# Attention key tiles of 128 rows per head, with the casts of q, k and v on VectorE and ScalarE

## The chip, the cores and the metric

The kernel runs on one core of a Trainium2 chip. The metric is device time in microseconds (us) of one launch. The engines are TensorE (PE, matmuls; its weight loads are PEld), VectorE (DVE), ScalarE (ACT), GpSimd (POOL) and SyncE (SP, which here only issues DMAs).

## The reference

Attention with a relative-position bias over 8 batch rows, 8 heads, 576 positions and head size 64; then a routed expert layer with 8 experts.

```python
scores = scale * np.matmul(q, k.transpose(0, 1, 3, 2))
...
bias = bias_table[bucket]            # bucket of |i - j|, 32 buckets, the last one from 128 on
scores = scores + bias.transpose(2, 0, 1)[None, :, :, :]
scores = scores - np.max(scores, axis=-1, keepdims=True)
attn = np.exp(scores)
attn = attn / (np.sum(attn, axis=-1, keepdims=True) + 1e-09)
return np.matmul(attn, v)
...
expert_idx = token_ids * np.int64(2654435761) % np.int64(E)
for e in range(E):
    h = np.maximum(x[expert_idx == e] @ w1[e], 0.0)
    out[expert_idx == e] = h @ w2[e]
```

q, k and v are float32 of shape (8, 8, 576, 64), w1 is (8, 512, 1024), w2 is (8, 1024, 512), and the output is float32 (4608, 512).

## The kernel before

There are two stages. The attention stage goes over 32 pairs of heads: a batch row and two heads, m and m + 4, whose 64 dimensions together fill the 128 partitions. The expert stage then goes over 8 experts with up to 640 tokens each.

**Attention, pair n.** load(n) (L176) brings q and k of the two heads as float32 on the SP queue, two rows of 64 to a packet of 512 bytes, four pairs ahead. cast_qk (L203) makes float16 of them on POOL. transpose_q (L321) and transpose_k (L337) turn them on PE in six blocks of 96 rows each, and VectorE copies the result out of PSUM: q as it is (L329), k into kz (L346). kz holds zeros where a key column belongs to the other head, so that one matmul over 128 partitions gives the scores of keys of both heads: a key tile of 128 columns is 64 keys of one head and 64 keys of the other, in an order where the even and odd positions of the sequence are kept apart.

The scores come out with keys on partitions and queries along the free dimension. scores(n, g) makes two key tiles at a time for g = 0 to 3 (L370, L374) and the last half tile for g = 4 (L385), into a PSUM tile ps of three banks with two buffers. ScalarE takes the exp (L378, L390) into att and atts. The bias is added as a factor: far from the diagonal the bias is one number per head, which cancels in the softmax, so only a band near the diagonal is multiplied, on VectorE (L411, and L417 for the last half tile), with ebd, the exp of the bias differences.

av_steps(n) multiplies att by va (L439): va holds v of both heads in float16 beside a column of ones each, 2 x 65 = 130 columns, with zeros in the rows of the other head. So 9 matmuls of 130 columns per tile of 128 queries, 45 per pair, give the numerators and the row sums; VectorE takes the reciprocals (L449) and scales into x_all (L450). The PSUM tiles px, pq and pk share two banks called aux. load_v (L188) brings v from the POOL queue, cast to float16 by the DMA, in packets of 64 values.

**Order.** All engines' orders in this stage are written out by hand. In the loop pass n, five score tiles of pair n alternate with 13, 14, 9 and 9 of the value matmuls of pair n - 1 on PE; transpose_k(n + 1) stands behind the first score tile and transpose_q(n + 2) behind the fourth. On VectorE the passes run: copy of k, band of the last half tile of pair n - 1, normalising of the first three query tiles, bands 0 and 1 of pair n, copy of q, band 2, normalising of the last two query tiles, band 3.

**The start.** The bias differences are made by a small matmul (bps) and an exp on ScalarE (ebsb), and written to DRAM by ScalarE's queue as t_f, shifted by one element per row (L535). Four DMAs on the SP queue read them back in diagonals as ebd (L549). z_init and va_init write zeros and ones on VectorE.

**Routing** is worked out on VectorE during passes 6 to 11. From pass 12 on, dispatch (L465) scatters finished rows of x_all to their expert's rows in DRAM (t_xperm) by indirect DMAs of POOL; the weights of the first two experts are loaded from POOL's queue in passes 20 to 28. route_load (L219) brings the token ids on SP in pass 4, and fill_table (L571) fills t_xperm on SP in passes 2 to 11. The last dispatches follow the last pair; then the expert stage loads its rows (L661), transposes them (L675), multiplies by w1 (L696), takes the relu (L702), multiplies by w2 (L714), and scatters the result (L722).

Of the kernel before, what the change touches and what calls it, by code (L numbers as in the profile page):

```python
# [11 lines left out]
F32 = mybir.dt.float32  # L12
# [19 lines left out]
def kernel(  # L32
# [11 lines left out]
    nc = tc.nc  # L44
# [63 lines left out]
    PW = 2 * FY + D // 2  # L108
    F_d = nc.dram_tensor("t5_f", [H * D + 1, PW], F16, kind="Internal")
# [36 lines left out]
    VW = 2 * (D + 1)  # L146
# [4 lines left out]
    with tc.tile_pool(name="at", bufs=1) as at, tc.tile_pool(  # L151
# [3 lines left out]
        def aux(shape, dtype, name):  # L155
# [4 lines left out]
        kz = [at.tile([P, NCH, 2, D], F16, name=f"kz{i}") for i in range(3)]  # L160
        va = [at.tile([P, NPAIR * NCH, VW], F16, name=f"va{i}")
              for i in range(2)]
        ebd = at.tile([P, NPAIR, 2, 2, WB], F16, name="ebd")
        te = at.tile([P, NGT], I32, name="te")
# [4 lines left out]
        qf, kf, qh, kh = {}, {}, {}, {}  # L169

        def load(n):
            b, m = pairs[n]
            for dst, src, name in ((qf, q, "qf"), (kf, k, "kf")):
                dst[n] = at.tile([PB, 2, NBLK, 2 * D], F32, name=name, bufs=4)
                for hh in range(2):
                    nc.sync.dma_start(  # L176
                        out=dst[n][:, hh, :, :],
                        in_=src[b, m + NPAIR * hh].rearrange(
                            "(k p c) d -> p k (c d)", k=NBLK, c=2
                        ),  # L180
                    )

        def load_v(b, m0, m1):
            for hh in range(2):
                for c in range(2):
                    r0 = D * hh + HD * c
                    c0 = hh * (D + 1)
                    nc.gpsimd.dma_start(  # L188
                        out=va[b % 2][r0 : r0 + HD, NCH * m0 : NCH * m1,
                                      c0 : c0 + D],  # L190
                        in_=bass.AP(
                            v.tensor,
                            (b * H + hh * NPAIR + m0) * S * D + c * D,
                            [[2 * D, HD], [D * D, NCH * (m1 - m0)], [1, D]],
                        ),
                    )

        def cast_qk(n, keng=None):
            for dst, src, name, eng in (
                (qh, qf, "qh", nc.gpsimd), (kh, kf, "kh", keng or nc.gpsimd)  # L200
            ):
                dst[n] = at.tile([PB, 2 * NBLK, 2, D], F16, name=name, bufs=3)
                eng.tensor_copy(  # L203
                    out=dst[n][:, :, :, :].transpose([0, 2, 1, 3]),
                    in_=src[n][:, :, :, :].rearrange(
                        "p h k (c d) -> p h (k c) d", c=2
                    ),
                )

# [122 lines left out]
        def transpose_k(n):  # L332
            pk = aux([P, S], F16, "pk")
            for k3 in range(NBLK):
                for c in range(2):
                    o = HALF * c + PB * k3
                    nc.tensor.transpose(  # L337
                        out=pk[:, o : o + PB],
                        in_=kh[n][:, 2 * k3 + c, :, :].rearrange(
                            "p h d -> p (h d)"  # L340
                        ),
                        identity=ident[:PB, :PB],
                    )
            z = kz[n % 3]
            for hh in range(2):
                nc.vector.tensor_copy(  # L346
                    out=z[D * hh : D * hh + D, :, hh, :].rearrange(
                        "p x (c u) -> p x c u", c=2
                    ),
                    in_=pk[D * hh : D * hh + D, :].rearrange(  # L350
                        "p (c x u) -> p x c u", c=2, u=HD
                    ),
                )
            ktz[n] = z

        def scores(n, g):
# [10 lines left out]
            if g < NDUO:  # L367
                for c in range(2):
                    kt = z[:, 2 * g + c, :, :].rearrange("p h u -> p (h u)")
                    nc.tensor.matmul(  # L370
                        out=ps[:, c, :QW], lhsT=kt, rhs=qt[:, :QW],
                        start=True, stop=True,
                    )
                    nc.tensor.matmul(  # L374
                        out=ps[:, 2, RW * c : RW * c + RW], lhsT=kt,
                        rhs=qt[:, QW:], start=True, stop=True,
                    )
# [4 lines left out]
            else:  # L382
                kt = z[:, 2 * NDUO, :, :].rearrange("p h u -> p (h u)")
# [11 lines left out]
        def band(n, g):  # L395
# [19 lines left out]
            else:  # L415
                a = ats[:, QW:].rearrange("p (o u) -> p o u", o=2)
                nc.vector.tensor_tensor(  # L417
                    out=a, in0=a, in1=ebd[:, m, 0, :, :UB], op=ALU.mult
                )

        def av_steps(n, done=None):
            b, m = pairs[n]
            att, ats = atts[n]
            vb = va[b % 2][:, NCH * m : NCH * m + NCH, :]
            for its in ((0, 1, 2), (3, 4)):
                px = aux([P, len(its), 2, D + 1], F32, "px")
                todo = [(ii, it, t) for ii, it in enumerate(its)
                        for t in range(2 * NDUO + 1)]
                for x, (ii, it, t) in enumerate(todo):
                    if t < 2 * NDUO:  # L430
                        g, c = t // 2, t % 2
# [434 lines left out]
```

The softmax here doesn't subtract the row's maximum and nothing guards it: scores larger than these inputs give would overflow.

## Time and profile before

| what | value |
|---|---|
| median of three runs | 420.94 us (417.95 to 426.08) |
| the profiled execution | 419.06 us, span 417.3 us |
| mean granted TensorE clock | 0.949 |
| PE busy | 344.7 us, 83% |
| DVE busy | 231.2 us, 55% |
| ACT busy | 206.8 us, 50% |
| POOL busy | 193.6 us, 46% |
| POOL casts of q and k (L203) | 63 of 0.86 to 0.88 us |
| value matmuls (L439) | 1440, 0.22 us each from start to landing |
| first band product | at 31.94 us |
| first rows of the first expert loaded | at 256.6 us |

Busy time counts an engine's instructions and not its waits. A matmul's duration is from its start to its last result; the next one starts earlier, so the spacing of starts tells what one costs. The slices of the page divide the span into 40 parts of 10.4 us; a digit is the busy share in tenths. The timelines list instructions in order of time with their duration, and in brackets the engine's idle time before them and who ended it. The chain of waits follows the work that ended last back from the end, at each step to what released it.

### The profile page before, as it was taken

To read this page: it belongs to the slowest core of one execution; us is meant where nothing else is said; L and a number is where in the kernel's file an instruction comes from. 1 tells how busy PE (TensorE), PEld (TensorE's weight loads), DVE (VectorE), ACT (ScalarE), POOL (GpSimd) and SP (SyncE) were. 2 spreads that over 40 slices of the span, in tenths; PEclk is the share of its full clock that TensorE was granted. 3 is DMA by queue.
4 is the path that set the end of the run, shared out by engine and by line. 5 is a ranking of instruction groups with operands and counts; after the bars stand their busy time and mean duration, and the time that the engine had idled before them with its cause. 6 is when DMAs were issued, how large, how long until landed. Compare 5 with 4: busy or idle time off the path is not lost.

```text
span 417.3 us, 8580 instructions
## 1 busy us (share of the span) xinstructions
PE 344.7 (83%) x3398; PEld 249.9 (60%) x3398; DVE 231.2 (55%) x550; ACT 206.8 (50%) x226; POOL 193.6 (46%) x232
## 2 busy tenths in 40 slices
PE   3407799799878989889897933999999999999990
PEld 1305588677667767768685832656566575656650
DVE  4108988989787998898886631132231414233120
ACT  1404678778768777858785810504233150513320
POOL 5504844644885778597824040051523334150321
PEclk9957999999999999989999985999999999999997
DMA  9999999999995979999971016089999899996211
GB/s 186 83 127 258 198 75 244 299 224 207 196 203 134 132 182 173 132 185 186 153 119 57 2 52 196 2 203 146 263 167 259 153 246 225 183 263 108 105 65 63
DMA packets 110002, 67.32 MB, mean 161 GB/s; under 512 B 50271, under 2 KB 101087, under 8 KB 109952
## 3 DMA queue, kind: packets, MB, share of 16 engines
q0 software_dynamic: 55552, 35.68, 63.4%
q1 hardware_dynamic: 53392, 30.33, 33.6%
q10 hardware_dynamic: 1008, 0.66, 1.1%
q8 instruction: 29, 0.48, 0.5%
q14 instruction: 21, 0.17, 0.2%
HBM read 68.18 MB, written 21.54 MB: 215 GB/s over the span
## 4 chain that ended last, share of the span: by engine, by line
PE 57%; DVE 16%; issue 10%; DMA 7%; ACT 5%; POOL 2%; SPq 0%; ACTq 0%; POOLq 0%; DVEq 0%
PE hps L696 17%; PE ops L714 17%; PE px L439 10%; DVE att L411 8%; PE ps L370 5%; ACT att L378 5%; PE ps L374 3%; DMA t_f<-ebsb 3%; DVE x_all L450 3%; PE xps L675 2%; DMA ebd<-t_f 2%; DVE qt L329 2%; POOL t_xperm L465 1%; DMA xpn<-t_xperm 1%; DVE kz L346 1%
## 5 line engine op out<-in xcount | busy, mean ns | idle before, releaser
L378 ACT ACTIVATE att<-ps 128x1152 f16<-128x1152 f32 x128 | 141.3, 1130 | 53.1 <-PE ps L374 43.3
L439 PE MATMUL px<-va,att 128*128 128x130 f16 x1280 | 101.7, 223 | 12.9 <-DVE x_all L450 9.8
L411 DVE TENSOR_TENSOR att<-att,ebd 128x512 f16<-128x512 f16 (+1 forms) x192 | 91.4, 516 | 20.4 <-DMA ebd<-t_f 20.3
L702 ACT ACTIVATE h<-hps 128x640 f16<-128x640 f32 x64 | 45.1, 704 | 112.7 <-PE hps L696 112.0
L439 PEld LDWEIGHTS <-att 128*128 128x128 f16 x1280 | 83.9, 99 | 22.0 <-DVE x_all L450 11.3
L370 PE MATMUL ps<-qt,kz 128*128 128x384 f16 x256 | 76.1, 336 | 11.9 <-ACT att L378 8.2
L696 PE MATMUL hps<-xpt,w1t 128*128 128x320 f16 x512 | 72.6, 303 | 0.0
L714 PE MATMUL ops<-w2t,h 128*128 128x512 f16 x320 | 72.7, 379 | 0.0
L722 POOL DMA_INDIRECT out_dram<-ok,xpn x40 | 39.2, 981 | 57.7 <-DVE ok L721 53.7
L374 PE MATMUL ps<-qt,kz 128*128 128x192 f16 x256 | 64.5, 252 | 0.4 <-issue 0.4
L696 PEld LDWEIGHTS <-w1t 128*128 128x128 f16 x512 | 50.6, 99 | 21.5 <-issue 0.2
L465 POOL DMA_INDIRECT t_xperm<-x_all,ds x40 | 41.3, 1033 | 38.7 <-DVE x_all L450 29.5
L679 DVE COPY xpt<-xps 128x640 f16<-128x640 f16 x32 | 15.1, 490 | 73.6 <-PE xps L675 72.7
L721 DVE COPY ok<-ops 128x512 f32<-128x512 f32 x40 | 27.7, 692 | 47.0 <-PE ops L714 47.0
L188 POOL DMA_DIRECT2D va<-in_v_dram x64 | 43.6, 697 | 21.2 <-PE ps L385 11.5
L714 PEld LDWEIGHTS <-h 128*128 128x128 f16 x320 | 30.7, 98 | 33.5
L203 POOL CAST qh<-qf 96x768 f16<-96x768 f32 x32 | 27.6, 861 | 35.4 <-DMA qf<-in_q_dram 26.6
L439 PE MATMUL px<-va,atts 128*128 128x130 f16 x160 | 35.5, 222 | 0.3 <-ACT atts L390 0.3
L374 PEld LDWEIGHTS <-kz 128*128 128x128 f16 x256 | 25.4, 99 | 16.2 <-issue 15.9
L370 PEld LDWEIGHTS <-kz 128*128 128x128 f16 x256 | 25.5, 100 | 13.0 <-DVE kz L346 2.4
L450 DVE TENSOR_TENSOR x_all<-px,rcp 128x384 f16<-128x384 f32 x64 | 31.4, 491 | 2.2
L203 POOL CAST kh<-kf 96x768 f16<-96x768 f32 x31 | 27.3, 881 | 10.8 <-PE pk L337 7.2
(52 smaller groups left out, 236.0 us busy)
## 6 DMA issues: line engine op xcount, KB each, us to landing
qf<-in_q_dram SPq DMA_DIRECT2D x64, 144.0 KB
kf<-in_k_dram SPq DMA_DIRECT2D x64, 144.0 KB
w1t<-in_moe_w_dram POOLq DMA_DIRECT2D x8, 1024.0 KB
w2t<-in_moe_w_dram POOLq DMA_DIRECT2D x8, 1024.0 KB
t_xperm<-zx SPq DMA_DIRECT2D x10, 514.0 KB
xpn<-t_xperm SPq DMA_DIRECT2D x8, 642.5 KB
va<-in_v_dram POOLq DMA_DIRECT2D x56, 72.0 KB
ebd<-t_f SPq DMA_DIRECT2D x4, 192.0 KB
```

What stands on the lines that cost most here:

```text
L188: nc.gpsimd.dma_start(out=va[b % 2][r0 : r0 + HD, NCH * m0 : NCH * m1, c0 : c0 + D], in_=bass.AP(v.tensor, (b * H + hh * NPAIR + m0) * S * ...
L203: eng.tensor_copy(out=dst[n][:, :, :, :].transpose([0, 2, 1, 3]), in_=src[n][:, :, :, :].rearrange("p h k (c d) -> p h (k c) d", c=2),)
L370: nc.tensor.matmul(out=ps[:, c, :QW], lhsT=kt, rhs=qt[:, :QW], start=True, stop=True,)
L374: nc.tensor.matmul(out=ps[:, 2, RW * c : RW * c + RW], lhsT=kt, rhs=qt[:, QW:], start=True, stop=True,)
L378: nc.scalar.activation(out=att[:, g, :, :], in_=ps[:, :, :QW], func=AF.Exp, bias=0.0, scale=scale,)
L411: nc.vector.tensor_tensor(out=a, in0=a, in1=ebd[:, m, :, :, a0 + w0 : a1 + w0], op=ALU.mult,)
L439: nc.tensor.matmul(out=px[:, ii, :, :].rearrange("p h d -> p (h d)"), lhsT=lhsT, rhs=vb[:, t, :], start=(x == 0), stop=(x == len(todo) - 1 ...
L450: nc.vector.tensor_tensor(out=x_all[:, b, its[0] : its[0] + ni, :DM].rearrange("p t (h m d) -> p t h m d", h=2, m=NPAIR)[:, :, :, m, :], i ...
L465: sc_in = nc.gpsimd.indirect_dma_start(out=xperm_d.ap()[:, :], out_offset=bass.IndirectOffsetOnAxis(ap=ds2[:, B * t + b : B * t + b + 1], ...
L696: nc.tensor.matmul(out=hps[:, nr, :NR], lhsT=w1h[:, kt, ts(ft, P)], rhs=xt[e][:, kt, ts(nr, NR)], start=(kt == 0), stop=(kt == NPT - 1),)
L702: nc.scalar.activation(out=h1[:, ft, :].rearrange("p (r n) -> p r n", r=NRC), in_=hps[:, :, :NR], func=AF.Relu, bias=0.0, scale=1.0,)
L714: nc.tensor.matmul(out=ops[:, :], lhsT=h1[:, ft, ts(kc, P)], rhs=w2h[:, ft, :], start=(ft == 0), stop=(ft == NFT - 1),)
```

## The change

Keys are kept in natural order in 128-row tiles of one head. The loads of k go by rows of 64 (256 bytes), four tiles per head and one half tile for the two heads together; v is loaded by the SP queue in the same way, as float32 (vf), together with q and k, and the last 64 rows of v for a whole batch row (load_vs). VectorE casts q and k (cast_q, cast_k), ScalarE casts v (cast_v) into vt, and POOL casts the last rows of v (cast_vs). kz becomes two straight stretches of 576 columns, one for each head, with zeros in the other head's 64 partitions; the scores of a full tile are of one head, and the two half tiles lie side by side in the middle and make one tile of both heads. The value matmuls of a tile multiply by the v of that head alone, 98 columns wide (v, a one, zeros), at two offsets in the 132-column result; the last half tile keeps all 132 columns. The bias table in DRAM has 128 rows per head instead of 64; its read-back is by head, in four DMAs, and four more bring the rows for the last half tile (ebs). The zeros and ones of vt and vs are written by POOL.

```diff
-    PW = 2 * FY + D // 2
-    F_d = nc.dram_tensor("t5_f", [H * D + 1, PW], F16, kind="Internal")
+    PW = 2 * FY
+    F_d = nc.dram_tensor("t5_f", [H * P + 1, PW], F16, kind="Internal")
...
+    HP = D + 2
+    VW = 2 * HP
+    VN = 98
+    VO = HP - (VW - VN)
...
         def load(n):
             b, m = pairs[n]
...
+            qf[n] = at.tile([PB, 2, NBLK, 2 * D], F32, name="qf", bufs=4)
+            vf[n] = at.tile([P, 2, NDUO, D], F32, name="vf", bufs=4)
+            z = kf[n % 4]
             for hh in range(2):
+                h = m + NPAIR * hh
...
+                nc.sync.dma_start(
+                    out=z[:, :NDUO, hh, :],
+                    in_=k[b, h, :NB4].rearrange("(t p) d -> p t d", p=P),
+                )
+            nc.sync.dma_start(
+                out=z[:D, NDUO, :, :],
+                in_=k[b, m::NPAIR, NB4:].transpose([1, 0, 2]),
+            )
+            for hh in range(2):
+                h = m + NPAIR * hh
+                nc.sync.dma_start(
+                    out=vf[n][:, hh, :, :],
+                    in_=v[b, h, :NB4].rearrange("(t p) d -> p t d", p=P),
+                )
...
+        def cast_q(n):
+            qh[n] = at.tile([PB, 2 * NBLK, 2, D], F16, name="qh", bufs=3)
+            nc.vector.tensor_copy(
...
+        def cast_k(n):
+            kh[n] = at.tile([P, NIT, 2 * D], F16, name="kh", bufs=3)
+            nc.vector.tensor_copy(
...
+        def cast_v(n):
+            nc.scalar.activation(
...
+                in_=vf[n][:, :, :, :], func=AF.Copy, bias=0.0, scale=1.0,
+            )
...
         def transpose_k(n):
+            pk = aux([P, S + PB], F16, "pk")
+            for o, t, w in [(0, NDUO, PB)] + [
+                (D + P * t, t, P) for t in range(NDUO)
+            ] + [(D + NB4, NDUO, PB)]:
+                nc.tensor.transpose(
+                    out=pk[:, o : o + w], in_=kh[n][:w, t, :],
+                    identity=ident[:w, :w],
+                )
             z = kz[n % 3]
+            nc.vector.tensor_copy(out=z[:D, :S], in_=pk[:D, D : D + S])
+            nc.vector.tensor_copy(out=z[D:P, S:], in_=pk[D:P, :S])
...
         def av_steps(n, done=None):
...
+                    if x is None:
+                        lhsT = ats[:, i_first[it] : i_first[it] + P]
+                        rhs, o, w = vs[b % 2][:, m, :], 0, VW
+                    else:
...
+                        o, w = (VW - VN) * hh, VN
+                        v0 = (NDUO * VN + VO) * hh - VO * hh + VN * t
+                        rhs = vb[:, v0 : v0 + VN]
                     nc.tensor.matmul(
+                        out=px[:, ii, o : o + w], lhsT=lhsT, rhs=rhs,
...
-        for cj in range(2):
+        for r in range(2):
             nc.scalar.dma_start(
                 out=bass.AP(
-                    F_d.ap().tensor, cj * HD * PW,
-                    [[D * PW, H], [PW + 1, HD], [1, 2 * FY]],
+                    F_d.ap().tensor, r * PW,
+                    [[P * PW, H], [2 * PW + 1, D], [1, 2 * FY]],
                 ),
...
         transpose_q(0)
         transpose_k(0)
-        cast_qk(1)
-        load(2)
+        cast_v(0)
+        cast_k(1)
+        cast_q(1)
+        for hh in range(2):
+            for o in range(2):
+                f0 = hh * P * PW + o * FY + MAXD // 2 - 1
+                nc.sync.dma_start(
+                    out=ebd[:, :, hh, o, :],
+                    in_=bass.AP(F_d.ap().tensor, f0,
+                                [[PW, P], [2 * P * PW, NPAIR], [1, WB]]),
+                )
+                nc.sync.dma_start(
+                    out=ebs[D * hh : D * hh + D, :, o, :],
+                    in_=bass.AP(F_d.ap().tensor, f0,
+                                [[PW, D], [2 * P * PW, NPAIR], [1, UB]]),
+                )
         load(2)
...
         load(3)
-        load_v(0, 1, NPAIR)
-        z_init(2)
-        cast_qk(2)
+        cast_vs(0)
+        cast_v(1)
+        cast_k(2)
+        cast_q(2)
...
             for g in range(NIT):
                 scores(n, g)
...
                 elif g == 1:
+                    if n + 2 < NP:
+                        cast_v(n + 2)
+                    if n > 0 and n + 2 < NP:
+                        cast_k(n + 2)
                     advance(av, 14)
                     band(n, 0)
                 elif g == 2:
+                    if n + 3 < NP:
+                        cast_q(n + 3)
                     advance(av, 9)
                     band(n, 1)
```

In the loop, cast_v(n + 2) stands between the second and third exp of a pair on ScalarE, cast_k(n + 2) ahead of the first normalising on VectorE, and cast_q(n + 3) between bands 0 and 1.

## The prediction

> **What bounds the kernel now.** I read the page's busy rows and slices first, then the chain of waits in order of time, then the timelines of single pairs. The page:
>
> ```profile
> PE 344.7 (83%) x3398; PEld 249.9 (60%) x3398; DVE 231.2 (55%) x550; ACT 206.8 (50%) x226; POOL 193.6 (46%) x232
> ...
> DVE  4108988989787998898886631132231414233120
> ```
>
> The shares mean little: in slices 4 to 20 (attention) VectorE (DVE) is as full as TensorE (PE), and in the expert stage after it only PE counts. Behind 257 us the diff touches nothing, so I price two stretches: the start, and the loop over pairs. The chain at the start:
>
> ```profile
> 9.40 11.86 DMA t_f<-ebsb
> ...
> 22.87 8.95 DMA ebd<-t_f
> 31.94 0.89 DVE att L411 x2
> ```
>
> The bias table goes to DRAM and back before the first band product (L411); till then nothing can go on. In the loop, one quiet pair and one disturbed pair:
>
> ```profile
> 120.10 2.61 DVE L411 TENSOR_TENSOR att<-att,ebd 128x512 f16<-128x512 f16 x2
> 120.94 0.84 POOL L203 CAST qh<-qf 96x768 f16<-96x768 f32 x1
> 121.72 0.84 POOL L203 CAST kh<-kf 96x768 f16<-96x768 f32 x1
> 123.31 0.64 PE L439 MATMUL px<-va,att 128*128 128x130 f16 x8 [2.14 <-DVE x_all L450]
> ```
>
> ```profile
> 214.48 0.32 PE L370 MATMUL ps<-qt,kz 128*128 128x384 f16 x1 [0.20 <-ACT att L378]
> ...
> 220.18 0.32 PE L370 MATMUL ps<-qt,kz 128*128 128x384 f16 x1 [0.20 <-ACT att L378]
> ```
>
> In the first, two band products that take 0.61 us elsewhere take 2.61 while POOL casts, and PE then idles 2.14 us for VectorE. Over the loop, band products that overlap no POOL work sit at their clean lengths; those beside casts and v-load issues hold an excess of 29 us in all, and those beside dispatch issues alone (47 of them) 0.07 us. In the second POOL casts nothing and the pair takes 5.70 us. My marker is the first exp of a pair on ScalarE (ACT): pair 1 at 35.49, pair 31 at 236.64, so 30 intervals of 6.70 on average; quiet ones are 5.70 or 6.03.
>
> **The start.** The table in DRAM grows from 512 to 1024 rows of 1024 B, from the same 8 partitions. Its 512 packets ran at a steady 48 per us from 10.5 to 20.9, also in the microseconds when nothing else moved; 1024 take 10.3 us more, so it lands at 31.6 instead of 21.3 (bounds +8 and +12). Reading back was 4 DMAs of 512 packets: 10.5 us from first issue to landing, partly beside v loads of the POOL queue that are gone. Now there are 8, with 1024 smaller packets more; SP issues them in 8 x 0.51 = 4.1 us. Bounds: 3072 packets at the best rate in that read (558 per us) and 1.5 us to land, 7 us; the read's mean rate (195 per us), 16 us. I take 10, nearer the good rate, since the small ones repeat rows and the v loads are gone: 42.
>
> load(2), which SP issued at 5.15, now stands behind these, and VectorE has cast_k(2) and cast_q(2) ahead of the first band product. Five DMAs of load(2) move 2.4 us of packets: 44.5. The two casts: 45.4. The first band product, then cast_q(3), which waits for load(3): 2.9 us more of packets, 47.4, and 0.5. From there band, q and k copies, the last score tile and pair 1's first scores take 2.7 us (3.55 before from the first band product): first exp of pair 1 at 50.6, which is +15 (12 to 21). ACT's cast_v(2) also waits here, for the v of load(2) at about 46, with exp 2 and exp 3 of pair 0 behind it; these are needed by 50, so it costs nothing unless load(2) is 3 us later still. PE idles here as it did before.
>
> **The loop, per pair.** PE: 40 of 45 attention-by-value matmuls shrink from 130 to 98 columns. They start every 0.058 us now; bounds are 0.058 (no gain) and 0.042 (96-column transposes, L321). I take 0.043, the nearest row. Four k transposes widen from 96 to 128 columns, +0.05 in all. PE's sum falls from 5.29 to 4.75.
>
> VectorE: the band, copy and normalising work starts back to back in 4.64 us per pair when clean (each starts 0.083 before its predecessor's recorded end: 0.416 long, next after 0.333). Added: cast_q, 0.556 long by the one cast VectorE did before (kh, 96x768 f32), so 0.47; cast_k, 128x640, between 0.46 and 0.56 long, I take 0.49, so 0.41. Sum 5.52. The copies into kz become straight, but q's straight copy of as many elements takes the same (453 against 452 ns): nothing. The 29 us of excess go with POOL's casts.
>
> ACT: cast_v, 128x512. Between the rows 128x576 (652 ns) and 128x1152 (1130) a line gives 0.60, or 0.50 of spacing; 0.70 at most (L702, 128x640). It stands between exp 1 and exp 2, and scores of the next pair wait for exp 3 because ps has two buffers. Relu and Exp share one table load in this trace; I take Copy to need none (another load costs 1.28).
>
> The quiet pair laid out from its first score matmul: second scores at 1.50, third at 2.81, exp 2 at 3.50, exp 3 ends 5.65, next pair 5.70. Changed: second scores at 1.50 + 0.05 - 12 x 0.015 = 1.37; exp 1 at 2.06; cast_v at 3.08; third scores at 2.50, so exp 2 could start at 3.19 but waits for cast_v: 3.58; exp 3 ends 5.73; next pair 5.78. VectorE's 5.52 fits with 0.26 to spare; what it is late with next is the normalising (L450) that frees PE's bank, due at 6.5 and done at 6.3. With three engines this close I add half of what quiet pairs scatter: 5.9.
>
> SP issues 7 loads a pair, 7 x 0.45 = 3.2 us, and runs 2.9 pairs ahead of the first cast. Its 13.4 us of token loads (L219) may make load(9) late: 1 us. The routing's 14 VectorE operations, 4.7 us, had cover; they find 0.26 a pair: 3 us. One stall of PE's own issue (223.7 to 226, then half clock) I keep: 3 us. The value rows of the last half tile (load_vs, cast_vs) are two small loads and two 64x256 POOL casts per batch row, one loop pass ahead of use: nothing, and a band product blocked by one, 0.5 us, if they meet. The zero fills and ones move from VectorE (2.0 us at 36.3) to POOL, which is then idle: they cost nothing at the start, because the table's wait hides them; cover gone, 2 us.
>
> Loads: k's packets go from 512 to 256 B and v's come by SP as 256 B, so 2304 of 256 B and 576 of 512 B per pair. The identity's load shows 256-B packets at 20 ns, q's 512-B ones take 29: (2304 x 20 + 576 x 29)/16 = 3.9 us per pair, under 5.9. The Trainium skill, "DMA: Bandwidth & Descriptors", Specifications, asks for 512 B and says smaller transfers are read, modified and written; taking that as a 256-B packet no cheaper than a 512-B one, it would be 5.2 us per pair and, by the sum in the second rival, about 428 (estimate). The measured 20 ns decides.
>
> VectorE's casts could also meet POOL's dispatch issues. The Trainium skill, "SBUF — State Buffer", Who interferes with whom, has casts in the two-port mode and GpSimd block each other; by it some 15% of 40 dispatches of 1 us meet a cast, 6 us at most. Band products beside dispatches lost nothing, so my sum has none.
>
> **Sum.** 30 x 5.9 = 177, + 3 + 3 + 1 = 184 against 201. Pair 31 starts at 50.6 + 184 = 234.6 instead of 236.6: -2. The last pair's 40 matmuls, uncovered: -0.6. Dispatch of the last rows, their landing and the first expert load (244 to 257) follow the last normalising as now, and the expert stage is as before. The profiled run took 419.06 (span 417.3), so 416.5, said as 417; the median of the runs shown, 420.94, is 1.9 above it, inside their scatter of 8.
>
> **Rivals.** A time must leave 412.5 to 429.4 to be over 2% off, which is about what a measurement of this kernel tells from no change.
>
> Both low ends: the table is back at 39, pair 1 starts at 47.6, pairs take 5.8, the PE stall does not recur: 47.6 + 174 + 3 = 224.6, -12, so 407. For it: the excess beside POOL is real and five pairs did 5.70. Against: VectorE's spare 0.26.
>
> Transfers become the bound, in the loop, at k's and v's 256-B packets. If they cost 32 ns, as v's do now in the POOL queue, a pair's loads take 5.65; 28 pairs 158, ten table fills 13, four weight loads 24, dispatches 12: 207 against 184, so 440. It decides from 26 ns up ((184 - 49)/28 = 4.8 us per pair). Against it: v's packets reached 890 per us, 18 ns an engine, between 204 and 206.
>
> 98 columns bring nothing: the change does not do what it says. Second scores at 1.55, third at 2.86, pairs 0.18 longer: +5.4, 422.
>
> The start is worse: the read at its mean rate, pair 1 at 56: 422.
>
> **How the numbers follow.** Forecast 0.41 at 417 (own range 412 to 423); low ends 0.23; transfers 0.24; no gain from columns 0.05; worse start 0.07. Same is 0.41 + 0.05 + 0.07 = 0.53. The range runs to 406, the low case, and to 434, inside the transfer case, of which it leaves out most.
>
> **What would show it.** Right: band products at 0.28 to 0.55 us throughout, the attention-by-value matmuls 0.043 apart, the first exp of pair 1 near 50, pairs of 5.8 to 6.0, ACT waiting less than 0.6 us a pair. Wrong: casts on VectorE that wait for kf or qf (transfers), a second table load on ACT, quiet pairs above 6.2, or the first band product before 40 or after 50.

## The result and the profile after

The changed kernel takes 437.93 us (median of 4 runs, 436.74 to 439.33), the kernel before beside it 419.44 (416.34 to 426.08). The ratio is 1.0468, 95% interval 1.0386 to 1.055: slower. The forecast was 417 with a range to 434, so the time lies above the range.

The profiled execution has a span of 436.0 us, 18.7 more than before. Two marks divide it, read from the trace as starts of the first exp of a pair on ScalarE:

| stretch | before | after | difference | forecast |
|---|---|---|---|---|
| start, to the first exp of pair 1 | 35.49 | 48.48 | +13.0 | +15 |
| pairs 1 to 9 | 54.48 | 50.67 | -3.8 | |
| pairs 9 to 31 | 146.67 | 156.38 | +9.7 | |
| both of these | 201.15 | 207.04 | +5.9 | -17 |
| rest | 180.66 | 180.48 | -0.2 | -0.6 |

The start and the rest went as forecast. The loop is 23 us longer than forecast, all of it behind pair 12. The page of the changed kernel, its busy line, the slices of VectorE and the granted clock:

```profile
PE 334.5 (77%) x3398; PEld 238.0 (55%) x3398; DVE 225.9 (52%) x608; ACT 219.7 (50%) x258; POOL 106.8 (24%) x135
...
DVE  4001699999953594898989561121413223142221
...
PEclk9999999999996697999999897699999999999997
```

VectorE is full in slices 6 to 11 and then falls to 5 and 3, with a granted clock of 0.6 to 0.7 in slices 13 and 14. Before, it had 7 to 9 through all of slices 4 to 20. Something new happens at 122 us.

The start, first on SyncE and then on VectorE:

```profile
31.79 0.38 SPq L602 DMA_DIRECT2D ebd<-t_f  x1
...
36.64 0.60 SPq L185 DMA_DIRECT2D qf<-in_q_dram  x1
```

```profile
41.72 0.49 DVE L234 CAST kh<-kf 128x640 f16<-128x640 f32 x1 [29.87 <-DMA kf<-in_k_dram]
42.13 0.55 DVE L225 CAST qh<-qf 96x768 f16<-96x768 f32 x1
42.60 0.41 DVE L439 TENSOR_TENSOR att<-att,ebd 128x512 f16<-128x512 f16 x1
44.80 0.56 DVE L225 CAST qh<-qf 96x768 f16<-96x768 f32 x1 [1.79 <-DMA qf<-in_q_dram]
```

The table is back in SP's hands at 31.79 (forecast 31.6), load(2) is issued behind the read, its casts start at 41.72, and cast_q(3) waits 1.79 us for load(3): the order of the forecast, some 3 us sooner.

A quiet pair on ScalarE, from one first exp to the next:

```profile
61.68 1.13 ACT L406 ACTIVATE att<-ps 128x1152 f16<-128x1152 f32 x1 [0.25 <-ACT atts L418]
63.02 1.13 ACT L406 ACTIVATE att<-ps 128x1152 f16<-128x1152 f32 x1 [0.20 <-PE ps L402]
64.04 0.62 ACT L240 ACTIVATE vt<-vf 128x512 f16<-128x512 f32 x1
...
67.49 1.13 ACT L406 ACTIVATE att<-ps 128x1152 f16<-128x1152 f32 x1 [0.25 <-ACT atts L418]
```

67.49 - 61.68 is 5.81, and pairs 3 to 5 and 10 to 12 take just that; the pair laid out had said 5.78. The new stretch, on POOL and on ScalarE:

```profile
134.40 0.98 POOL L498 DMA_INDIRECT t_xperm<-x_all,ds  x1 [0.28 <-POOL vs L218]
135.68 0.97 POOL L498 DMA_INDIRECT t_xperm<-x_all,ds  x1 [0.30 <-issue]
...
143.32 1.09 POOL L498 DMA_INDIRECT t_xperm<-x_all,ds  x1 [0.30 <-issue]
```

```profile
136.75 1.13 ACT L406 ACTIVATE att<-ps 128x1152 f16<-128x1152 f32 x1 [1.46 <-issue]
137.77 0.62 ACT L240 ACTIVATE vt<-vf 128x512 f16<-128x512 f32 x1
145.99 2.15 ACT L406 ACTIVATE att<-ps 128x1152 f16<-128x1152 f32 x2 [7.59 <-remote]
148.03 0.66 ACT L418 ACTIVATE atts<-ps 128x576 f16<-128x576 f32 x1
```

POOL issues eight dispatches in a row, 1.28 us apart, and ScalarE stands idle for 7.59 us with no releaser that the profile can name. The two pairs of this stretch take 11.6 and 15.24 us. TensorE and VectorE in the same microseconds:

```profile
137.60 0.29 PE L472 MATMUL px<-vs,atts 128*128 128x132 f16 x1
...
138.13 0.25 PE L402 MATMUL ps<-qt,kz 128*128 128x192 f16 x1
...
143.30 0.43 PE L358 MATMUL pq<-ident,qh 96*128 96x96 f16 x6 [4.03 <-issue]
```

```profile
142.45 0.20 DVE L482 RECIPROCAL rcp<-px 128x6 f32<-128x6 f32 x1 [6.08 <-issue]
142.68 0.56 DVE L483 TENSOR_TENSOR x_all<-px,rcp 128x384 f16<-128x384 f32 x1
```

The scores that the exp at 145.99 reads were done at 138.38, and the value products that the reciprocal at 142.45 reads at 137.89: ScalarE and VectorE learn of them 7.6 and 4.6 us late. TensorE itself is told in time: its transposes of q start at 143.30, 0.06 us behind the x_all that they wait for (142.68 + 0.56), and wherever behind 100 us its score matmuls stood idle for an exp, they start 0.05 us after it. So it is TensorE's results that are told late; the trace shows no late word to TensorE. In the whole trace, from 45 us on, 19 instructions of ScalarE and VectorE stand idle for over 0.5 us beside a finished result of TensorE, 7.6 us at most. The recorded semaphore updates alone can't tell this: in this trace some records are missing (503 for 539 updating instructions of VectorE, 241 for 258 of ScalarE), and the time to the next record is then not a delay.

Before, dispatches went in twos with POOL's casts of q and k between them (first at 103.0, after at 123.0), and the longest such wait was 3.1 us, beside the one burst of five.

### The profile page after: what moved, and what is told of

Its sections match the earlier page's. It is cut to its first block, busy times and chain, and to the rows that moved or that the text cites. A ratio compares the mean times of both kernels' runs of the same rounds, so it can differ in the third digit from the quotient of the medians.

```text
span 436.0 us, 8653 instructions
## 1 busy us (share of the span) xinstructions
PE 334.5 (77%) x3398; PEld 238.0 (55%) x3398; DVE 225.9 (52%) x608; ACT 219.7 (50%) x258; POOL 106.8 (24%) x135
## 5 line engine op out<-in xcount | busy, mean ns | idle before, releaser
L398 PE MATMUL ps<-qt,kz 128*128 128x384 f16 x256 | 78.1, 344 | 34.7 <-ACT att L406 30.7
L472 PE MATMUL px<-vt,att 128*128 128x98 f16 x1280 | 84.6, 211 | 2.8 <-issue 1.4
L472 PEld LDWEIGHTS <-att 128*128 128x128 f16 x1280 | 72.4, 101 | 9.0 <-issue 2.8
L439 DVE TENSOR_TENSOR att<-att,ebd 128x512 f16<-128x512 f16 (+1 forms) x192 | 68.4, 385 | 0.7 <-ACT att L406 0.5
L498 POOL DMA_INDIRECT t_xperm<-x_all,ds x40 | 40.0, 1001 | 82.1 <-DVE x_all L483 40.4
L218 POOL CAST vs<-vsf 64x256 f16<-64x256 f32 x16 | 7.7, 484 | 128.2 <-DMA vsf<-in_v_dram 100.8
L358 PE MATMUL pq<-ident,qh 96*128 96x96 f16 x192 | 14.5, 215 | 29.0 <-DVE qt L366 20.3
L472 PE MATMUL px<-vs,atts 128*128 128x132 f16 x160 | 36.1, 225 | 0.5 <-ACT atts L418 0.3
L240 ACT ACTIVATE vt<-vf 128x512 f16<-128x512 f32 x32 | 19.8, 623 | 31.1 <-DMA vf<-in_v_dram 31.1
L234 DVE CAST kh<-kf 128x640 f16<-128x640 f32 x32 | 15.6, 487 | 34.7 <-DMA kf<-in_k_dram 34.6
```

The source lines that it names most:

```text
L240: nc.scalar.activation(out=vt[n % 4][:, :].rearrange("p (h y) -> p h y", h=2)[:, :, : NDUO * VN].rearrange("p h (t x) -> p h t x", t=NDUO) ...
L398: nc.tensor.matmul(out=ps[:, hh, :QW], lhsT=kt, rhs=qt[:, :QW], start=True, stop=True,)
L439: nc.vector.tensor_tensor(out=a, in0=a, in1=ebd[:, m, :, :, a0 + w0 : a1 + w0], op=ALU.mult,)
L472: nc.tensor.matmul(out=px[:, ii, o : o + w], lhsT=lhsT, rhs=rhs, start=(y == 0), stop=(y == len(todo) - 1), skip_group_check=True,)
L498: sc_in = nc.gpsimd.indirect_dma_start(out=xperm_d.ap()[:, :], out_offset=bass.IndirectOffsetOnAxis(ap=ds2[:, B * t + b : B * t + b + 1], ...
```

## The experiments

Theory: dispatches issued back to back on POOL hold up what the other engines tell each other (by the lines above, what TensorE tells), and the casts that the change took from POOL had kept them apart (bursts). Rivals: casts on VectorE and dispatches on POOL block each other (port); small packets and SP's longer queue (transfers); the start alone matters (start).

The runs came in five groups, each on one chip beside the kernel before. In groups 1, 2 and 4 the kernel before takes 409.9 to 411.5 us, and no instruction of ScalarE or VectorE in the loop of any trace waits more than 0.4 us for a finished result of TensorE; in group 3, group 5 and the first comparison it takes 417.8 to 419.5, and the longest such wait of a trace is 1.8 to 8.2 us. I call these the prompt and the late groups; ratios are to the kernel before in the same group. The record gives groups 1 and 3 the same chip number (8), one prompt and one late. Where the expectations speak of updates up to 11 us late, that is the time to the next record that was kept; the longest wait in that profile is 7.6 us. The table gathers what was measured, from starts of first exps as above.

| run | group | us | ratio (95%) | first exp of pair 1 | mean of pairs 9 to 31 |
|---|---|---|---|---|---|
| before | first, late | 419.4 | 1 | 35.49 | 6.67 |
| after | first, late | 437.9 | 1.047 (1.039, 1.055) | 48.48 | 7.11 |
| e1_paced | 1 | 416.8 | 1.013 (1.010, 1.017) | 49.07 | 6.29 |
| e2_no_dispatch | 1 | 412.8 | 1.004 (1.000, 1.007) | 48.53 | 5.93 |
| e3_before_bursts | 1 | 415.3 | 1.009 (1.005, 1.013) | 36.38 | 6.39 |
| e4_before_no_dispatch | 1 | 405.8 | 0.987 (0.983, 0.991) | 36.33 | 5.95 |
| r_after | 2 | 420.3 | 1.027 (1.021, 1.032) | 48.48 | 6.27 |
| r_before | 2 | 410.5 | 1.004 (1.000, 1.007) | 35.83 | 6.19 |
| e5_loads_first | 2 | 416.8 | 1.016 (1.011, 1.022) | 48.28 | 6.27 |
| e6_two_queues | 2 | 415.9 | 1.013 (1.007, 1.020) | 45.65 | 6.29 |
| e7_pool_casts | 3, late | 429.8 | 1.024 (1.018, 1.030) | 47.55 | 6.70 |
| e8_132_columns | 3, late | 443.5 | 1.057 (1.051, 1.064) | 49.13 | 7.19 |
| e9_no_weights | 3, late | 440.4 | 1.051 (1.044, 1.057) | 48.91 | 7.11 |
| e10_quarters | 3, late | 424.0 | 1.013 (1.005, 1.020) | 47.84 | 6.40 |
| e1_paced_2 | 4 | 417.6 | 1.015 (1.011, 1.019) | 48.58 | 6.20 |
| e3_before_bursts_2 | 4 | 416.5 | 1.012 (1.007, 1.016) | 35.10 | 6.39 |
| e11_table16 | 4 | 407.9 | 0.990 (0.986, 0.994) | 39.96 | not read |
| e12_singles | 4 | 403.5 | 0.978 (0.973, 0.983) | 41.09 | 5.94 |
| e3_before_bursts_3 | 5, late | 445.2 | 1.068 (1.061, 1.075) | 35.88 | 7.72 |
| e12_singles_2 | 5, late | 410.7 | 0.984 (0.977, 0.990) | 40.95 | 6.27 |

**Dispatches spaced, left out, and bunched (group 1).**

```diff
 # e1: the dispatches of pass n stand behind cast_k(n + 2), each after
+            nc.gpsimd.tensor_copy(out=scr[:1, :8], in_=kh[n + 2][:1, 0, :8])
 # e2 (after) and e4 (before)
-                        dispatch(*waiting.pop(0))
+                        waiting.pop(0)
 # e3 (before)
-            if n >= 12:
-                for _ in range(2):
+            if n in (12, 16, 20, 24, 28, 30):
+                for _ in range(8):
```

> The changed kernel, with each of the up to two dispatches of a pass made to wait for its pass: ahead of each, POOL copies 8 elements of kh(n + 2), which VectorE writes in the middle of pass n. So no dispatch can run ahead of or catch up with the loop in a burst. Bursts theory (indirect DMAs issued back to back on POOL hold up what the other engines tell each other): the intervals of 7 to 15 us at passes 12 to 30 fall to 5.8 to 6.6, pair 31 starts 15 to 25 us sooner, 413 to 423 us. Port theory (VectorE's casts and POOL's dispatches block each other whenever they overlap): as many overlaps as now, 432 to 440. Transfers theory (256-byte packets and the load queue): 434 to 440. Start theory (the 13 us of the start are all that matters): 436 to 440.

> The changed kernel without the 35 dispatches of the loop (left out: the rows of the first seven batch rows are not scattered to their experts; the last five dispatches and all of the expert stage's work stay). Bursts theory and port theory alike: all pairs after the routing take 5.8 to 5.9 us, pair 31 starts at 225 to 230 instead of 255.5, 406 to 412 us. Transfers theory: the load queue and its 256-byte packets are as before, the long intervals stay, 430 to 438 us. Start theory: 434 to 438.

> The kernel before, with its loop dispatches gathered: up to 8 at once in passes 12, 16, 20, 24, 28 and 30 instead of two a pass; nothing else is changed, so there are no casts on VectorE but the first, and no 256-byte loads of k. Bursts theory: intervals of 8 to 15 us appear beside each gathered group, 430 to 445 us. Port theory: the dispatches meet no cast on VectorE, 418 to 424 us. Transfers theory: 418 to 424 us.

> The kernel before without the 35 dispatches of the loop (left out: the rows of the first seven batch rows are not scattered). It says what dispatches spaced by POOL's casts cost. Bursts theory: the one group of five back to back (218 to 225 us) goes, and with it 3 us, the pairs cost little otherwise: 412 to 418 us. Port theory: 416 to 420. If even spaced dispatches hold up the other engines, below 410.

e1 and e2 came out about as the bursts theory had it (e2 0.8 us above its range), but e3 did not: groups of five to eight dispatches cost the kernel before 1%, and the pairs beside the first four groups took 5.70 to 6.20 us (longer ones, up to 9.50, stand between them). e4 took 405.8, below the 412 to 418 of the theory and in the range set for spaced dispatches that cost too, but its kernel before was 8 us faster than in the first comparison as well. In all four traces no wait for a finished result of TensorE was over 0.4 us. So the first three could not be read without the changed kernel in such a group. One reading stands by itself: without dispatches, pairs 9 to 31 take 5.95 us in the kernel before, with POOL's casts all in place, and 5.93 in the changed one. Moving the casts, and the narrow matmuls, gain 0.5 us in 22 pairs.

**The two kernels once more, and the start (group 2).** r_after and r_before are the kernels as they are. e5 and e6:

```diff
+        load(2)
+        load(3)
         for hh in range(2):
             for o in range(2):
                 f0 = ...                      # read-back of the table
-        load(2)
-        load(3)
 # e6 has this besides
-            nc.scalar.dma_start(
+            (nc.scalar if r == 0 else nc.gpsimd).dma_start(
```

> The changed kernel as it is, beside the kernel before on one chip. In the first three kernels of the study the recorded semaphore updates came 0.015 us after their instructions throughout, while in the two first profiles they came up to 11 us late beside POOL's dispatches; so that lateness may belong to the chip or the moment and not to back-to-back dispatching. If it belongs to the chip: updates on time here, no interval of 10 us beside the dispatches of passes 12 to 15, 1.010 to 1.025 of the kernel before. If it belongs to this kernel's bursts (which pacing, or leaving the dispatches out, had taken away): the late updates are back, 1.035 to 1.055.

> The kernel before as it is, for its trace beside the other runs of this study. Lateness of the chip: updates on time, pairs of 5.7 and 6.03 us through most of the loop, though POOL casts as ever; pair 31 starts at 228 to 232 us instead of 236.6. Lateness of the dispatches: updates up to 2 us late beside each pair of dispatches as in the first profile, pair 31 at 235 to 238.

> The changed kernel with load(2) and load(3) issued on SP ahead of the read-back of the table instead of behind it. Start theory: the casts of pair 2 no longer stand ahead of the first band product waiting for their loads; the first exp of pair 1 moves from 48.5 to 44 to 46 us, and 2 to 5 us come off the time. If the read-back itself sets the end (the last ebs lands at 40 to 42 either way): 0 to 1 us.

> As the run before, and the second half of the table write goes by POOL's queue instead of ScalarE's. If the 48 rows per us are the limit of one queue's or eight engines' reading of 8 partitions, the two halves overlap: table in DRAM near 21 us instead of 31.6, first exp of pair 1 at 36 to 39, 7 to 11 us off the time of the changed kernel. If they are a limit of the source partitions or of the DRAM rows: as the run before.

The changed kernel is 1.027 here and not 1.047, just above the 1.010 to 1.025 expected for updates on time: 2% of the time belong to what is different in the late groups. The windows of both profiles of the same kernel, columns start:end, length, busy time with count of PE, PEld, DVE, ACT and POOL, granted clock, DMA share and GB/s. First the late one, then the prompt one:

```profile
122.00:131.00 9.00, 5.28 (x75) 4.13 (x74) 4.39 (x12) 4.22 (x5) 6.00 (x6) 0.99 1.09 237
131.00:137.60 6.60, 4.65 (x41) 3.92 (x41) 3.61 (x11) 3.66 (x4) 3.51 (x5) 0.50 1.19 238
137.60:144.50 6.90, 2.50 (x36) 1.89 (x34) 2.01 (x5) 0.79 (x2) 5.29 (x6) 0.99 1.16 274
144.50:151.40 6.90, 3.85 (x28) 2.91 (x28) 3.49 (x12) 3.82 (x4) 0.00 (x0) 0.51 0.19 54
```

```profile
122.00:131.00 9.00, 7.62 (x112) 6.23 (x111) 8.69 (x27) 8.30 (x11) 5.35 (x5) 1.00 1.06 238
131.00:137.60 6.60, 5.91 (x91) 4.93 (x89) 6.38 (x18) 6.15 (x7) 3.58 (x5) 1.00 0.95 232
137.60:144.50 6.90, 6.21 (x94) 5.24 (x93) 6.60 (x20) 6.25 (x8) 5.38 (x6) 1.00 1.03 250
144.50:151.40 6.90, 6.21 (x94) 5.21 (x92) 6.59 (x20) 6.45 (x9) 1.54 (x2) 1.00 0.95 230
```

POOL does the same in both (six and eight dispatches in a row from 123 and 134, or 124 and 136). In the late profile ScalarE runs 2 instructions where it runs 8 in the other, and beside each stall the clock is halved for some 7 us. Both move 232 to 274 GB/s beside the bursts, so the bytes are not what differs.

In the prompt pair of profiles the 12.8 us between spans (407.1 and 419.9) are +12.65 at the start, -2.4 in pairs 1 to 9, +1.7 in pairs 9 to 31 and +0.9 behind. So there the start is the whole loss. e5 shows why it can't be mended by order alone:

```profile
37.44 0.37 SPq L604 DMA_DIRECT2D ebd<-t_f  x1
```

With the loads ahead, the table's write shares the DMA engines with them and lands 5.6 us later (37.44 for 31.84 in r_after); pair 1 starts at 48.28 for 48.48, where I had expected 44 to 46. The 1% that e5 is better by lies in pairs 1 to 9 of its profile (49.5 for 53.0), where two profiles of the changed kernel itself differ by 2.3 us (50.67 and 53.00), so it is not shown to be the order's doing. In e6, POOL's half of the write is issued only when the first has landed, so the halves do not overlap and the question asked went unanswered (pair 1 at 45.65, where 36 to 39 was expected):

```profile
21.05 1.04 POOL L586 DMA_DIRECT2D t_f<-ebsb  x1 [17.33 <-DMA t_f<-ebsb]
```

**One part undone, and the weights (group 3, late).**

```diff
 # e7: cast_q, cast_k
-            nc.vector.tensor_copy(
+            nc.gpsimd.tensor_copy(
 # e8
-    VN = 98
+    VN = 132
 # e9: load_w1, load_w2 of passes 20 to 28 left out, instead
+            if n == 2:
+                for w in w1t + w2t:
+                    nc.gpsimd.memset(w[:, :, :], 0.0)
 # e10: as e5, and for load_w1, load_w2 of passes 20 to 28
+            if 12 <= n < 28:
+                load_wq(n - 12)               # 256 KB each
```

> The changed kernel with one part undone: cast_q and cast_k on POOL instead of VectorE, at the same places in the order; all else (tiles of 128 rows, 98 columns, loads, v on ScalarE) is kept. The step of my sum: POOL's casts stretch the band products beside them and pairs pay for it, so pairs 9 to 31 grow from 6.27 to 6.7 or more, 428 to 436 us where the changed kernel takes 420. The theory that the stretched band products had cover all along: band products of 0.41 us show up at 0.8 to 1.3 beside the casts, and pairs 9 to 31 stay within 0.15 us of the changed kernel's, 416 to 424 us.

> The changed kernel with value matmuls of 132 columns instead of 98 (VN = 132, one place). If PE's sum sets the pair: 40 x 0.015 = 0.6 us more for each, 30 pairs, +18 us. By the pair laid out from its waits (12 value matmuls stand between two score tiles on the path): 0.16 to 0.18 us more for each, quiet pairs of 5.97 to 6.0 instead of 5.81, +4 to +6 us. If ScalarE with the cast of v sets it: quiet pairs stay at 5.81, 0 to +1 us.

> The changed kernel without the weight loads of passes 20 to 28 (the first two experts' weights are zeros, written by POOL in pass 2, instead of 4 MB from DRAM; dispatches are kept). If the long intervals of passes 24 to 30 are q, k and v loads held up behind weight loads: they fall to 5.8 to 6.2 and 7 to 10 us come off the changed kernel. If they are made by the dispatches alone: 0 to 2 us. On a chip with late semaphore updates the long intervals of passes 12 to 15 would show as well.

> load(2) and load(3) ahead of the read-back of the table, and the first two experts' weights loaded in quarters of 256 KB, one in each of passes 12 to 27, instead of four whole loads of 1 MB. If whole weight loads hold up the loads of the pairs: the intervals of 8 to 10 us go, 3.5 us from the start and 5 to 8 from the loop, 409 to 413 us, no slower than the kernel before. If it is the bytes and not their bunching: 415 to 418, as with the loads alone.

The numbers expected were for a prompt group, so these are compared with the first profile of the changed kernel, 1.047. **e7** is the step of my sum undone, and it is faster, 1.024: pairs 9 to 31 take 6.70 for 7.11. Its page's band products, and ahead of them those of the changed kernel:

```profile
L439 DVE TENSOR_TENSOR att<-att,ebd 128x512 f16<-128x512 f16 (+1 forms) x192 | 68.4, 385 | 0.7 <-ACT att L406 0.5
```

```profile
L439 DVE TENSOR_TENSOR att<-att,ebd 128x512 f16<-128x512 f16 (+1 forms) x192 | 81.0, 461 | 29.0 <-DMA ebd<-t_f 28.1
```

POOL's casts do stretch them, by 12.6 us in all, but the quiet pairs 3 to 5 take 5.81 in both: the stretch is covered. And the casts stand between the dispatches, which now go in twos some 4 us apart; the longest wait for a finished result of TensorE is 1.8 us, where the changed kernel had 7.6. (One pair of 13.76 us, which both theories missed, is a cast: it stands behind a first dispatch that waits until 125.75.)

**e8**: quiet pairs of 5.98 instead of 5.81, as laid out by the 12 matmuls on the path:

```profile
74.36 1.13 ACT L406 ACTIVATE att<-ps 128x1152 f16<-128x1152 f32 x1 [0.25 <-ACT atts L418]
...
80.35 1.13 ACT L406 ACTIVATE att<-ps 128x1152 f16<-128x1152 f32 x1 [0.25 <-ACT atts L418]
```

**e9**: pairs 9 to 31 as slow as with the weights, 7.11, so in a late group the weight loads cost nothing beside the dispatches. **e10**: a weight load of 256 KB on POOL stands between two dispatches and the next two, which start 3.3 to 3.7 us later; passes 12 to 17 take 37.4 us where the changed kernel takes 56.5, the ratio falls from 1.047 to 1.013. I had expected its gain from the weights; by e9 and the waits (3.3 us at most) it is the spacing. That load(2) and load(3) also stand first in it moves pair 1 by 0.6 us (47.84 for 48.48).

**Bunching alone, and a remedy (groups 4 and 5).** e1_paced_2, e3_before_bursts_2 and e3_before_bursts_3 are the same kernels again, to meet a late group. e11 and e12:

```diff
 # e11: e10 with the table written from 16 partitions
-                    [[P * PW, H], [2 * PW + 1, D], [1, 2 * FY]],
+                    [[P * PW, 2 * H], [2 * PW + 1, D], [1, FY]],
 # e12: e11 with one dispatch behind cast_k(n + 2), one behind transpose_q(n + 2)
+                nc.gpsimd.tensor_copy(out=scr[:1, :8], in_=x)   # x: kh, then qt
+                dispatch(*waiting.pop(0))
```

> The paced kernel of the first run once more, for a chip on which the semaphore updates come late (there the changed kernel takes 1.047 of the kernel before, elsewhere 1.027). Bursts theory, on such a chip: delays of at most 2 to 3 us instead of 11, no interval of 10 us in passes 12 to 24, 1.010 to 1.030. If bunching does not matter and each dispatch costs its own delay: 1.035 to 1.05. On a chip with updates on time: 1.013 as before.

> The kernel before with its dispatches gathered in groups of up to 8, once more, for a chip with late updates. Bursts theory, on such a chip: delays of 6 to 11 us beside each group, as in the changed kernel, though VectorE casts nothing here; intervals of 9 to 15 us, 1.02 to 1.06. If the casts on VectorE or the 256-byte packets are needed for it: 1.005 to 1.015. On a chip with updates on time: 1.009 as before.

> The kernel of the quarters run (load(2) and load(3) first, weights in quarters), and the bias table written from 16 partitions, 256 entries each, instead of from 8 with 512: the same two DMAs, 2048 packets of 512 bytes instead of 1024 of 1024. If the bytes that each source partition gives set the time of the write: 9 to 11 us instead of 21.5, the table in DRAM at 19 to 22, the first exp of pair 1 at 36 to 40 instead of 47.8, 8 to 11 us off the quarters run: 400 to 404 where the kernel before takes 410, 413 to 416 where it takes 420. If the number of packets sets it: 0 or slower.

> As the run with 16 partitions, with the two dispatches of a pass set apart: one behind the cast of k, one behind the copy of q, each after a POOL copy of 8 elements that makes it wait. Bursts theory, on a chip with late updates: delays of 1.3 us at most, which two score buffers cover in part; 3 to 6 us faster than that run. On a chip with updates on time: within 2 us of it.

> The kernel before with its dispatches gathered in groups of up to 8, a last time for a chip with late updates. Bursts theory, on such a chip: delays of 6 to 11 us beside each group though VectorE casts nothing; 1.02 to 1.06. If the casts on VectorE or the 256-byte packets are needed for it: 1.005 to 1.015. On a chip with updates on time: 1.009 to 1.012, as twice before.

> The version with the dispatches set apart singly, the weights in quarters and the table from 16 partitions, for a chip with late updates. Bursts theory, on such a chip: delays of at most 1.3 to 2 us, passes 12 to 28 of 5.8 to 6.5 us, 0.97 to 0.99 of the kernel before, where the changed kernel was 1.047. If each dispatch costs its delay wherever it stands: 1.0 to 1.02. On a chip with updates on time: 0.978 as before.

Group 4 was prompt: e1 and e3 came out as in group 1. Group 5 was late, and there the kernel before with bunched dispatches takes 1.068, with no cast on VectorE in its loop and no load of 256 bytes a row but v's, as ever. Its POOL and ScalarE beside the first eight, late (e3_before_bursts_3) and then prompt (e3_before_bursts):

```profile
105.71 1.08 POOL L465 DMA_INDIRECT t_xperm<-x_all,ds  x1 [0.17 <-DMA kf<-in_k_dram]
...
114.83 1.22 POOL L465 DMA_INDIRECT t_xperm<-x_all,ds  x1 [0.30 <-issue]
```

```profile
104.38 1.13 ACT L378 ACTIVATE att<-ps 128x1152 f16<-128x1152 f32 x1 [0.24 <-PE ps L374]
...
111.55 1.13 ACT L378 ACTIVATE att<-ps 128x1152 f16<-128x1152 f32 x1 [1.83 <-PE ps L385]
117.33 0.65 ACT L390 ACTIVATE atts<-ps 128x576 f16<-128x576 f32 x1 [4.65 <-remote]
117.88 1.12 ACT L378 ACTIVATE att<-ps 128x1152 f16<-128x1152 f32 x1
```

```profile
106.39 1.08 POOL L465 DMA_INDIRECT t_xperm<-x_all,ds  x1 [0.17 <-issue]
...
115.63 1.12 POOL L465 DMA_INDIRECT t_xperm<-x_all,ds  x1 [0.30 <-PE px L439]
```

```profile
105.06 1.13 ACT L378 ACTIVATE att<-ps 128x1152 f16<-128x1152 f32 x1 [0.24 <-PE ps L374]
...
111.09 1.13 ACT L378 ACTIVATE att<-ps 128x1152 f16<-128x1152 f32 x1 [0.24 <-PE ps L374]
```

The same eight dispatches: a pair of 13.5 us (104.38 to 117.88) in one, of 6.03 in the other. That settles bunching against the port and the transfers; the long stalls need both, bunched dispatches and a late group. e12 puts a POOL copy that waits for the loop ahead of each dispatch, and takes 0.978 and 0.984 of the kernel before in either kind of group, a part of which is its earlier start (pair 1 at 41 for 48). In the late one its waits are at most 1.7 us, as expected, but for one of 3.1 beside the last four dispatches of the loop, which start only 1.33 us apart, and dispatches still cost: pairs 9 to 31 take 6.27 for 5.94. In the prompt one e12 is 4.4 us faster than e11, where within 2 was expected and nothing is told late; no run says where these come from.

Of e11, the write's packets moved at 172 per us of 512 bytes (88 GB/s) instead of 49 of 1024 (50 GB/s), in e12's trace of the same write. But the second DMA began some 7 us after the first had ended, so the table was back at 30.0 there and 29.3 in e11 instead of the 19 to 22 expected. Pair 1 started at 39.96, at the edge of 36 to 40, and the 407.9 us lie above the 400 to 404 expected.

## Why the prediction was wrong

**Start: right.** +13.0 for +15; 1024 rows at 48 to 50 per us, the read, load(2) behind it and the wait of cast_q(3) are in the trace one by one. The read was 3 us quicker than taken.

**The changed pair: right.** 5.81 for 5.78 laid out and 5.9 taken; value matmuls 0.043 us apart; casts of 0.487, 0.557 and 0.623 us for 0.49, 0.556 and 0.60; one table load. e8 prices the columns at 0.17 us a pair, as in the rival's 0.18.

**What the loop of before is made of: wrong, and this is the step that failed.** I wrote "The 29 us of excess go with POOL's casts" and set 5.9 for 6.70 a pair. The excess on VectorE is real and went, but hardly any of it was on the path: e4 keeps the casts and its pairs take 5.95, and e7 brings them back at no cost in quiet pairs. What pairs 9 to 31 had above 5.95 (0.72 us of the 6.67 in the first profile) went with the dispatches, 22 x 0.72 = 16 us, and the change keeps every dispatch. (The 5.95 is of a prompt group; no run leaves the dispatches out in a late one. In prompt groups the same difference is 6.19 - 5.95, 5 us.)

**The dispatches: wrong.** "Band products beside dispatches lost nothing, so my sum has none" looked at how long an instruction takes beside a dispatch, and not at how late its end is told. In the changed kernel, against the 5.93 us of e2, they cost 22 x (7.11 - 5.93) = 26 us in a late group and 22 x (6.27 - 5.93) = 7.5 in a prompt one, where leaving them out gave 420.3 - 412.8 = 7.5 too (groups 2 and 1). The stall of 223.7 to 226 that I kept as "PE's own issue" stands beside the one burst of five in the kernel before: the exp at 225.90 starts 3.1 us after its scores are done. That taking work from POOL would let dispatches catch up in bursts was nowhere in the forecast. Why the dispatches begin 20 us later than before is only argued: POOL's first one waits for the last fill of t_xperm, which SP issues at 117.35, behind its longer start and seven loads a pair.

With 26 in the place of nothing for the dispatches, the loop comes to 30 x 5.81 + 3 + 26 = 203 against 207.04 measured; that is no test, since the 26 was read from the same pairs.

**The rivals.** The transfers' 440 is near the number, and not by its mechanism: 256-byte packets took 18 ns in the median, and the loop's quiet passes show no cast waiting for a load. The Trainium skill, "DMA: Bandwidth & Descriptors", Specifications, asks for 512 bytes. The estimate of 428 that I made from it took a packet of 256 bytes to be as dear as one of 512, and here they took 18 and 27 ns. In prompt groups some long pairs of passes 24 to 30 (7 to 10 us in r_after) do have cast_q waiting for qf; without dispatches (e2) none is over 6.8 us, and whether the weight loads take part there was not tried. The Trainium skill's "SBUF — State Buffer", Who interferes with whom, has VectorE's casts in the two-port modes and GpSimd block each other; no run here shows in which mode these casts ran. Dispatches took 1.00 us on average with VectorE's casts in the loop and 1.03 before, so nothing of the 6 us is seen on POOL's side.

**Still open.** What makes a group late: by the record's numbers the same chip was prompt in group 1 and late in group 3, so it is not the chip alone, and nothing in the profiles says more. Nor do they show what in a dispatch holds up TensorE's results and not those of the others. And e1 in prompt groups is 1.2% better than the changed kernel though its pairs 12 to 17 take the same 34.9 us; its profile is better in pairs 1 to 9 only, where it changes nothing.

## What to carry to other kernels

Before work is taken from an engine that also issues DMAs, look at what that work spaces: with nothing to wait for, the queued issues run back to back. A stretched instruction counts only if its end is waited for; take the suspected cause away in one run (here, the dispatches) before the excess is booked on it. And when idle time has no releaser in the profile, find the instruction whose result is awaited and compare its end with the waiter's start; a record of a semaphore update that is missing is no proof that the update came late.

## What the runs showed of the hardware

- Beside back-to-back indirect DMAs of POOL, 1.28 us apart, ScalarE and VectorE stood idle beside finished results of TensorE for up to 7.6 us (8.2 in e8) in three of six comparisons, and for at most 0.4 us in the others, for the same kernels. TensorE was told in time throughout (0.05 us behind the exps it stood idle for). With two casts of POOL between every two dispatches (e7) the longest wait was 1.8 us.
- In the changed kernel's first profile, idle stretches of 3.24 and 4.03 us on TensorE (129.71 to 132.95, 139.27 to 143.30) went with some 7 us each at a granted clock of 0.50 (131 to 137.6, 144.5 to 151.4).
- A write from 8 partitions to DRAM in packets of 1024 bytes ran at 50 GB/s, 133 ns a packet; from 16 partitions in packets of 512 at 88 GB/s, 64 ns a packet.
